# A Nyström attention, an ELU feed-forward and a top-2 expert layer on one core: the written-out order of the work before the experts' weights is replaced

## The chip, the core and the metric

The kernel runs on one core of a Trainium2 chip. The metric is the device time of one execution in microseconds. The core has a matrix engine (PE, with its weight loads shown apart as PEld), a vector engine (DVE), an activation engine (ACT), a general engine (POOL) and SP, which here only issues transfers.

## What is computed

Four batches of eight heads with 576 tokens each go through a Nyström attention with 32 landmarks, then all 2304 tokens through a feed-forward layer with an ELU, then through a noisy top-2 choice of eight experts. Cut to what matters:

```python
q_lm, k_lm = q.reshape(B,H,32,18,64).mean(3), k.reshape(B,H,32,18,64).mean(3)
A, Bm, C = softmax(q @ k_lm.T), softmax(q_lm @ k_lm.T), softmax(q_lm @ k.T)
Z = Bm.T / (norm1(Bm) * norminf(Bm) + 1e-6)
for _ in range(6):
    Z = 2 * Z - Z @ Bm @ Z
x = A @ Z @ C @ v                      # 2304 x 512
h = x @ w_in                           # 512 -> 2048
x = where(h > 0, h, exp(min(h, 0)) - 1) @ w_out
logits = x @ w_gate + log1p(exp(x @ w_noise)) * noise
# the two largest of 8 experts, softmax weights, relu(x @ w1[e]) @ w2[e]
```

## The kernel before

Everything up to the first expert is written as short commands in one long string, `ORDER`; `do` splits it and calls one small function for each word. The string is the program: each engine carries out its instructions in the order in which the words stand, and waits at an instruction until what it needs is there. Nothing reorders them later. The experts 1 to 7 that follow are an ordinary loop and no part of this.

The words are read so. A word with a colon belongs to the attention of one batch, as `1:nm.0` for batch 1. Its stages are the loads (`q`, `k`, `v`; `q.0` is the first four heads), the sums over 18 tokens that make the landmarks (`lmmm`, on PE at line 339 for batch 0), their transposes (`ltr`), the three score products (`asmm`, `bmm`, `csmm`), their softmax steps on DVE, ACT and POOL, and the inverse. The inverse starts with `nmm`, `nval`, `sqmm` and `y0`, then takes five Newton steps: `nm.i` is a product on PE (line 483), `sqout` copies half of it on ACT, `uout` adds the other half on DVE (line 571), and `nm.i+1` needs both. `umm.5` and `uout.5` close it, `ybd` spreads it, `cv` is the product of the third softmax with `v` (line 548), `zcv` (line 582) joins both, and `gmm.0` to `gmm.3` (line 645) multiply that with `w_in`. `ghi` and `glo` store the result as two float16 halves `G`.

The feed-forward layer takes the tokens in six chunks of 512, 256 and four times 384. `L1.c.f` is the first product of chunk `c` and hidden block `f` (line 678, six float16 products). The ELU of one block is five words: `X` (exponential, ACT), `T` (cut at 1 and minus 1, on ACT or DVE), `S` (scale and maximum, DVE, line 706), `H` (first float16 half, ACT), `O` (second half, on DVE or POOL, line 711). `L2.c.f.t` is the second product for 128 tokens (line 718). The last letter of `T` and `O` names the engine:

```python
    if part == "T":
        x.append(S_H if e is V else -S_H)
        if e is V:
            V.tensor_scalar(x[1], x[1], 1.0, 1.0, op0=ALU.min, op1=ALU.subtract)
        else:
            act(x[1], x[1], AF.Relu, scale=-1.0, bias=1.0)
    if part == "O":
        e.tensor_tensor(out=HT[c, f][:, 1], in0=x[1], in1=HT[c, f][:, 0], op=ALU.subtract)
```

`wi` and `Wl` load blocks of `w_in` and `w_out` of 512 KB, and `I.j.0` to `I.j.3`, `Wa`, `Wb` turn them into the number forms that the products use, on ACT, DVE and POOL. `nz`, `cl`, `fill` and `facc` load noise and gate weights and clear two buffers in DRAM. `YA`, `YV` and the words that begin with `R` are the choice of experts, `PD` and `P` load and split the weights of expert 0, and the words that begin with `E`, `W`, `LX` or `X` without the ELU's form are the experts' first stage. `F.n` is a warm-up: `warm(n)` issues products of a constant tile (`hot`) of `n` times 128 columns into a bank that nobody reads, up to 512 columns at a time (line 691). A transfer waits in SP's queue until the buffer that it writes is free and until the transfer eight before it has landed.

Of the kernel before, what the change touches and what calls it, by code (L numbers as in the profile page):

```python
# [56 lines left out]
0:xtp.0.1.0 0:asmax.0 0:bmm I.5.2 Wl.1 0:csmm.0 I.4.3 0:bmax 0:xth.0.1.0 0:xtp.0.1.2 F.16 0:bex 0:csmax.0 wi.14 wi.7
I.3.3 0:assub.0.G 0:bnorm 0:nmm Wa.0.2 F.15 0:nval 0:csexp.0 Wa.1.0 Wa.5.0 Wb.4.0.V F.15 0:xth.1.1.2 Wa.1.1 0:sqmm.0
Wa.5.1 I.1.1 Wa.1.2 I.5.0 0:sqout.0 wi.10 0:xth.0.1.2 nz.3.1 Wa.5.2 0:y0 Wa.1.3 I.7.1 Wl.3 0:csmm.1 F.16 Wa.5.3 F.3
0:xtp.0.1.1 Wa.3.0 0:asexp.0 0:csmax.1 wi.12 0:assum.0 Wa.0.3 nz.1.1 I.14.0 Wb.4.1.V F.9 0:nm.0 0:sqout.1 0:uout.0 wi.8  # L60
0:xth.0.1.1 0:csexp.1 0:etrans.1 0:nm.1 0:sqout.2 Wl.7 0:uout.1 wi.11 Wa.7.0 0:asmm.1 Wl.2 Wa.3.1 0:cssum I.11.0 I.1.0
0:v 0:etrans.2 Wa.3.2 0:etout.2 I.1.2 Wb.0.0.V 0:etrans.0 0:nm.2 0:sqout.3 0:astr.1 0:uout.2 Wa.2.0 nz.3.3 nz.2.2 nz.1.0
0:asmax.1 F.11 1:q.0 0:etout.0 Wb.1.0.V 0:nm.3 0:sqout.4 0:uout.3 0:nm.4 0:sqout.5 nz.3.0 0:asmul.0.G 0:assub.1.V I.10.1
F.9 0:uout.4 I.8.0 I.10.2 I.7.2 Wa.3.3 I.7.0 I.12.0 1:q.1 Wa.2.1 Wa.7.1 Wa.2.2 Wb.1.1.V wi.9 0:etout.1 Wa.2.3 0:umm.5
I.7.3 Wb.3.0.G 0:cv 0:asexp.1 0:asback.0 I.1.3 0:uout.5 1:lmmm.0.0 0:ybd.V 0:cvout 0:assum.1 0:ashi.0 0:zcv 0:asmul.1.G
F.14 0:zout F.8 0:aslo.0.G 0:asback.1 0:gmm.0 0:ghi.0.0 0:ghi.0.1 0:ashi.1 Wa.7.2 0:glo.0.1 0:aslo.1.G I.5.3 1:lmmm.0.1
0:glo.0.0 Wb.0.1.V Wb.2.0.V I.9.0 1:xhi.0.0 1:lmadd.0 Wb.5.0.V L1.0.0 X.0.0 1:v T.0.0.A L1.0.1 1:xlo.0.0 1:k.0 0:gmm.1
wi.13 X.0.1 Wb.3.1.G S.0.0 T.0.1.A H.0.0 wi.15 1:k.1 S.0.1 I.9.1 nz.3.2 L1.0.2 I.8.1 1:lhi.0 O.0.0.V L2.0.0.1 L1.0.3
H.0.1 L2.0.0.3 X.0.2 L2.0.0.0 1:xhi.0.1 I.11.1 L2.0.0.2 cl Wb.2.1.V Wa.7.3 0:ghi.1.1 Wb.5.1.V O.0.1.V 1:xlo.0.1 T.0.2.A
I.9.2 I.9.3 L2.0.1.3 nz.0.1 S.0.2 0:ghi.1.0 1:xhi.1.0 0:glo.1.0 X.0.3 H.0.2 L2.0.1.2 I.8.2 Wl.6 T.0.3.A 0:glo.1.1 S.0.3  # L70
L2.0.1.0 1:lmsum.1.0.V nz.0.2 Wb.7.0.V H.0.3 L2.0.1.1 L1.0.5 O.0.2.G I.8.3 Wb.7.1.V Wa.6.0 1:llo.0 L1.0.4 L2.0.2.2
O.0.3.G 1:xlo.1.0 I.15.0 X.0.4 X.0.5 I.10.0 L2.0.2.3 L2.0.2.0 1:ltr.0 T.0.4.A I.11.2 I.11.3 I.15.1 T.0.5.A S.0.4
1:xtr.0.0 S.0.5 H.0.4 1:lmsum.1.1.V L2.0.2.1 1:lcp.0.A L2.0.3.2 I.10.3 Wl.8 L2.0.3.0 L1.0.6 1:xtr.1.0 Wa.6.1 O.0.4.G
0:gmm.2 H.0.5 L1.0.7 X.0.6 0:ghi.2.1 L2.0.3.1 O.0.5.V 1:lhi.1 I.15.2 T.0.6.A X.0.7 Wa.6.2 0:glo.2.1 0:ghi.2.0 T.0.7.A
nz.0.0 1:xhi.1.1 L2.0.4.2 L2.0.3.3 Wa.8.0 L2.0.4.1 I.15.3 S.0.6 L2.0.5.1 0:glo.2.0 Wa.6.3 nz.0.3 Wb.6.0.V 1:csmm.0
I.14.1 Wa.8.1 1:xlo.1.1 H.0.6 L2.0.4.3 S.0.7 L2.0.5.2 L2.0.4.0 L1.0.9 Wl.12 Wl.9 1:csmax.0 Wb.6.1.V H.0.7 L1.0.8 consts
1:xtr.1.1 O.0.6.G 1:csexp.0 Wa.12.0 L2.0.5.3 L2.0.6.2 I.13.0 L2.0.5.0 1:llo.1 X.0.9 T.0.9.A L2.0.6.0 I.12.1 Wa.9.0
1:ltr.1 Wa.8.2 Wa.12.1 Wl.13 O.0.7.V I.13.1 X.0.8 nz.1.3 Wa.9.1 L2.0.7.2 I.12.2 1:lcp.1.A I.13.2 1:bmm L2.0.6.3 T.0.8.A
I.14.2 L2.0.7.3 I.13.3 Wa.8.3 1:bmax S.0.8 fill.0 Wl.10 1:csmm.1 Wl.11 I.12.3 I.14.3 L2.0.7.0 Wa.9.2 1:csmax.1 Wa.9.3
1:bex 1:csexp.1 Wb.8.0.V L2.0.6.1 H.0.8 Wa.13.0 L1.0.11 1:asmm.0 S.0.9 Wl.14 1:bnorm 1:astr.0 L2.0.7.1 1:etrans.0 1:nmm  # L80
1:nval L1.0.10 Wb.8.1.V 1:etout.0 1:sqmm.0 Wa.10.0 O.0.8.G 1:y0 1:etrans.2 Wb.9.0.V 1:sqout.0 L2.0.8.1 Wa.10.1 H.0.9
# [1343 lines left out]
```

## Time and profile before

| | |
|---|---|
| median of three runs | 785.49 us (784.63 to 786.11) |
| the profiled execution, its own time | 790.36 us |
| its span, first to last instruction | 788.7 us |
| mean granted clock of PE | 0.988 |
| PE busy | 761.0 us, 96% |
| DVE busy | 615.3 us, 78% |
| ACT busy | 427.0 us, 54% |
| POOL busy | 276.1 us, 35% |

The span is the stretch between the first and the last instruction; the execution's own time has a little around it. Busy time is counted from the records of each engine, and a product's recorded end is modelled, so a busy PE can still have small pauses. The granted clock is 1.00 at 2.4 GHz and 0.50 at 1.2 GHz. All times in the rows below count from the start of the span.

### The profile page before, as it was taken

To read this page: it belongs to the slowest core of one execution; us is meant where nothing else is said; L and a number is where in the kernel's file an instruction comes from. 1 tells how busy PE (TensorE), PEld (TensorE's weight loads), DVE (VectorE), ACT (ScalarE), POOL (GpSimd) and SP (SyncE) were. 2 spreads that over 40 slices of the span, in tenths; PEclk is the share of its full clock that TensorE was granted. 3 is DMA by queue.
4 is the path that set the end of the run, shared out by engine and by line. 5 is a ranking of instruction groups with operands and counts; after the bars stand their busy time and mean duration, and the time that the engine had idled before them with its cause. 6 is when DMAs were issued, how large, how long until landed. Compare 5 with 4: busy or idle time off the path is not lost. (4 is left out here: it accounts for less than half of the span.)

```text
span 788.7 us, 17580 instructions
## 1 busy us (share of the span) xinstructions
PE 761.0 (96%) x6991; PEld 447.1 (57%) x6992; DVE 615.3 (78%) x1350; ACT 427.0 (54%) x821; POOL 276.1 (35%) x303
## 2 busy tenths in 40 slices
...
GB/s 342 340 181 213 168 306 213 42 176 186 239 249 135 92 93 52 163 78 99 82 81 105 172 203 134 141 198 44 242 96 220 117 99 224 54 238 27 77 265 65
DMA packets 136200, 123.19 MB, mean 156 GB/s; under 512 B 102891, under 2 KB 105963, under 8 KB 136016
## 3 DMA queue, kind: packets, MB, share of 16 engines
...
## 5 line engine op out<-in xcount | busy, mean ns | idle before, releaser
L718 PE MATMUL y<-wout,g 128*128 128x512 f16 x864 | 205.3, 380 | 0.9 <-DVE g L711 0.8
L1161 PE MATMUL ey<-w,eh 128*128 128x512 f16 x768 | 167.2, 379 | 0.0
L1187 POOL DMA_INDIRECT acc<-eo,tk x35 | 71.1, 2031 | 205.8 <-ACT eo L215 97.5
L718 PEld LDWEIGHTS <-g 128*128 128x128 f16 x864 | 80.6, 98 | 92.3 <-issue 6.5
L1161 PEld LDWEIGHTS <-eh 128*128 128x128 f16 x768 | 75.1, 98 | 89.1
L678 PE MATMUL h<-AT,G 128*128 128x192 f16 (+3 forms) x768 | 108.5, 287 | 2.3 <-DVE e L706 2.2
L678 PEld LDWEIGHTS <-G 128*128 128x128 f16 x768 | 64.1, 98 | 46.6 <-issue 10.6
L711 POOL TENSOR_TENSOR g<-e,g 128x384 f16<-128x384 f32 (+2 forms) x45 | 44.5, 988 | 128.3 <-ACT g L215 118.2
L215 ACT ACTIVATE eh<-c 128x300 f16<-128x300 f32 x112 | 47.7, 453 | 62.9 <-DVE c L1083 58.0
L215 ACT ACTIVATE g<-e 128x384 f16<-128x384 f32 (+2 forms) x96 | 49.2, 520 | 49.8 <-DVE e L706 28.4
L215 ACT ACTIVATE e<-h 128x384 f32<-128x384 f32 (+2 forms) x96 | 46.2, 485 | 42.7 <-PE h L678 20.6
L706 DVE SCALAR_TENSOR_TENSOR e<-e,h 128x384 f32<-128x384 f32 (+2 forms) x96 | 51.6, 548 | 14.2 <-ACT e L215 12.1
L215 ACT ACTIVATE eo<-ey,ws 128x512 f32<-128x512 f32 (+3 forms) x60 | 32.4, 540 | 52.8 <-PE ey L1161 39.7
L903 POOL DMA_INDIRECT xs<-rows,pos x36 | 37.7, 1048 | 53.4 <-DVE mcum L887 25.4
L942 DVE SCALAR_TENSOR_TENSOR w<-ew,w 128x1024 f16<-128x1024 f32 x36 | 43.9, 1243 | 15.8 <-ACT w L215 12.0
L1066 PE MATMUL eb<-tx,wpC 128*128 128x300 f16 x336 | 47.4, 291 | 0.0
L1095 DVE SCALAR_TENSOR_TENSOR eh<-c,eh 128x300 f16<-128x300 f32 x112 | 46.3, 469 | 1.0
L711 DVE TENSOR_TENSOR g<-e,g 128x384 f16<-128x384 f32 (+2 forms) x51 | 30.2, 598 | 18.7 <-ACT g L215 18.4
L1066 PEld LDWEIGHTS <-wpD 128*128 128x128 f16 x336 | 32.8, 98 | 12.1 <-issue 2.0
L1066 PEld LDWEIGHTS <-wpB 128*128 128x128 f16 x336 | 32.9, 98 | 10.0
L1066 PEld LDWEIGHTS <-wpC 128*128 128x128 f16 x336 | 32.8, 97 | 10.1
L1083 DVE TENSOR_TENSOR c<-eb,u 128x300 f32<-128x300 f32 x84 | 37.0, 468 | 0.9 <-PE eb L1066 0.8
...
## 6 DMA issues: line engine op xcount, KB each, us to landing
...
```

The lines of the kernel that those rows point to most:

```text
L215: return A.activation(o, i, f, **kw)
L678: T.matmul(p[:, c0:c0 + n], GT[b, f // 8][:, g, x, fs], AT[b][:, g, y, o:o + n], start=(i == 0), stop=(i == 5))
L706: V.scalar_tensor_tensor(x[1], x[1], x[2], x[0], op0=ALU.mult, op1=ALU.max)
L711: e.tensor_tensor(out=HT[c, f][:, 1], in0=x[1], in1=HT[c, f][:, 0], op=ALU.subtract)
L718: T.matmul(YP[c, t], h[:, x, 128 * t:128 * t + 128], WOUT[f][:, y], start=(f == 0 and i == 0), stop=(f == 15 and i == 2))
L903: n = nc.gpsimd.indirect_dma_start(out=xs[:, :], out_offset=bass.IndirectOffsetOnAxis(ap=R["pos"][:, i // 2, i % 2:i % 2 + 1], axis=0), in ...
L942: V.scalar_tensor_tensor(dst[1][:, ks, :], t, scale, dst[0][:, ks, :], op0=ALU.mult, op1=ALU.subtract)
L1066: T.matmul(p, w_op(e, w, s, k, f), x_op(e, x, t, k), start=(i == 0 and k == 0), stop=(i == 2 and k == 1))
L1083: V.tensor_tensor(out=o, in0=EB[n, f], in1=EU[a, f], op=ALU.add)
L1095: V.scalar_tensor_tensor(lo, o, 0.0, hi, op0=ALU.max, op1=ALU.subtract)
L1161: T.matmul(p, EH[e, f][:, x, 128 * j:128 * j + 128], W2T[e][y][:, f, :], start=start, stop=stop)
L1187: nc.gpsimd.indirect_dma_start(out=acc[:, :], out_offset=bass.IndirectOffsetOnAxis(ap=TK[e][:live(j), j:j + 1], axis=0), in_=EO[e, j], in_ ...
```

## The change

Only the string `ORDER` differs. All words but the warm-ups are the same, and each stands once, so the same arithmetic is done. What differs is the order of the words up to the load and split of expert 0's weights, the engine letter of a part of the `T` and `O` words, and the warm-ups. Sixteen warm-up words of together 226 times 128 columns (60 products) stand before, seven of together 115 (30 products) after: `F.30`, three `F.16`, `F.15`, `F.14`, `F.8`. Of the engine letters, in sum one `T` goes from ACT to DVE and one `O` from POOL to DVE; in the last chunk it is one `T` and two `O`. From `RE.3` in the fifth chunk on, the order of the words is the same but for the engine letters.

```diff
 ORDER = """
-wi.0 F.30 0:k.0 Wl.4 I.0.0 0:q.0 Wa.4.0 F.16 F.16 0:xtp.1.0.0 0:xtp.1.0.2 wi.2 I.0.1 0:xth.1.0.0 I.0.2 0:lmmm.1.0 Wa.4.1
...
+0:q.0 F.30 wi.6 0:xtp.0.0.0 0:k.0 wi.2 wi.0 0:q.1 Wl.4 I.0.1 0:lmmm.0.0 I.2.1 wi.3 0:xtp.1.0.2 F.16 Wa.4.1 0:k.1
...
```

The first place is SP at the start of the program: which transfers are issued first. `k_127`, `q_133`, `q_181`, `k_192` are the four halves of batch 0 before, in this order. First before, then after:

```order
L1238 DMA wi_116<-in_moe_w_in_dram 128x1024
L224 DMA k_127<-in_k_dram 128x1152
L265 DMA wo_129<-in_moe_w_out_dram 128x1024
L224 DMA q_133<-in_q_dram 128x1152
L1238 DMA wi_153<-in_moe_w_in_dram 128x1024
L224 DMA q_181<-in_q_dram 128x1152
L1238 DMA wi_185<-in_moe_w_in_dram 128x1024
L224 DMA k_192<-in_k_dram 128x1152
```

```order
L224 DMA q_116<-in_q_dram 128x1152
L1238 DMA wi_127<-in_moe_w_in_dram 128x1024
L224 DMA k_133<-in_k_dram 128x1152
L1238 DMA wi_135<-in_moe_w_in_dram 128x1024
L1238 DMA wi_137<-in_moe_w_in_dram 128x1024
L224 DMA q_139<-in_q_dram 128x1152
L265 DMA wo_141<-in_moe_w_out_dram 128x1024
L1238 DMA wi_135<-in_moe_w_in_dram 128x1024
L224 DMA k_167<-in_k_dram 128x1152
```

The second half of `k` has moved from the eighth to the ninth transfer, one block of weights further back; the second half of `q` is the sixth in both.

The second place is PE at the end of batch 0's inverse. `nb` holds the Newton products, `l1b` the closing ones (`umm.5` at line 483, `zcv` at line 582), `pcv` is `cv`, the rows at line 339 are landmark sums of batch 1, and `pg` is `gmm.0`. First before, then after:

```order
L483 MATMUL nb_194<-R_570 32x64 x8
L691 LDWEIGHTS hot
L691 MATMUL warm<-hot 128x512
...
L483 MATMUL l1b_159<-R_581 32x32 x8
L548 MATMUL pcv_618<-v_515,ET_559 32x64 x8
...
L339 MATMUL nb_673<-q_557,ident 128x128 x9
L582 MATMUL l1b_159<-Yd_683,CV_685 64x64 x4
L691 LDWEIGHTS hot
...
L645 MATMUL pg_709<-win_131,Z_701 32x512
```

```order
L483 MATMUL nb_145<-R_531 32x64 x8
L548 MATMUL pcv_562<-v_445,ET_515 32x64 x8
...
L483 MATMUL l1b_213<-R_555 32x32 x8
L339 MATMUL nb_654<-q_415,ident 128x128 x9
L582 MATMUL l1b_213<-Yd_650,CV_639 64x64 x4
L339 MATMUL nb_654<-q_550,ident 128x128 x9
L645 MATMUL pg_693<-win_143,Z_676 32x512
```

The product with `v` now stands ahead of `umm.5`, the warm-ups of this stretch are gone but for two that now stand behind `gmm.0`, and the second landmark sum of batch 1 has come ahead of `gmm.0`.

The third place is PE in batch 1's Newton steps, which lie between the feed-forward products of chunk 0 (`h` and `y`). `pa` is `asmm.1`. First before, from the second to the fourth product of the chain, then after:

```order
L431 MATMUL pa_1443<-T_1346,lT_743 32x288
L483 MATMUL pu_1482<-R_1434 32x64 x8
L483 MATMUL pu_1494<-R_1491 32x64 x8
L678 LDWEIGHTS G_956
L678 MATMUL h_13_1505<-AT_690,G_956 128x512
...
L483 MATMUL pu_1516<-R_1503 32x64 x8
```

```order
L678 MATMUL h_12_1427<-AT_553,G_912 128x512
L483 MATMUL pu_1440<-R_1383 32x64 x8
L548 MATMUL pcv_1456<-v_642,ET_1283 32x64 x8
...
L483 MATMUL pu_1517<-R_1453 32x64 x8
L718 LDWEIGHTS g_10_1378
L718 MATMUL y_800<-wout_1130,g_10_1378 128x512
...
L483 MATMUL pu_1551<-R_1532 32x64 x8
```

Two Newton products that stood back to back now have `cv` between them, and the next two have four groups of feed-forward products between them. On DVE, in the same steps, this is what stands between the additions `R` of line 571 that the products wait for; first before, then after:

```order
L571 TENSOR_TENSOR R_1434<-pu_1425,R_1328 128x2x32
L259 TENSOR_SCALAR woc_1244<-wo_1137 128x512
L605 TENSOR_TENSOR ax_1287<-ax_1287,amx_1290 128x576
L260 SCALAR_TENSOR_TENSOR wo_1137<-wo_1137,woc_1244 128x512
L260 SCALAR_TENSOR_TENSOR wo_1220<-wo_1220,woc_1385 128x512
L596 STREAM_TRANSPOSE ax_1478<-pa_1442 128x288
L596 STREAM_TRANSPOSE ax_1478<-pa_1443 128x288
L571 TENSOR_TENSOR R_1491<-pu_1482,R_1434 128x2x32
```

```order
L571 TENSOR_TENSOR R_1383<-pu_1365,R_1315 128x2x32
L601 TENSOR_REDUCE amx_1174<-ax_1171 128x18
L596 STREAM_TRANSPOSE ax_1434<-pa_1399 128x288
L596 STREAM_TRANSPOSE ax_1434<-pa_1400 128x288
L605 TENSOR_TENSOR ax_1171<-ax_1171,amx_1174 128x576
L554 SCALAR_TENSOR_TENSOR cs_1080<-cs_1080 128x2
L555 RECIPROCAL cs_1080<-cs_1080 128x2
L259 TENSOR_SCALAR woc_1360<-wo_1139 128x512
L292 SCALAR_TENSOR_TENSOR wout_1130<-wo_1062,wout_1130 128x512
L260 SCALAR_TENSOR_TENSOR wo_1139<-wo_1139,woc_1360 128x512
L571 TENSOR_TENSOR R_1453<-pu_1440,R_1383 128x2x32
```

The transpose of `pa` (line 596), on which the second product of the chain also waits because it frees a bank, has come from the sixth to the second place behind the first addition, and the weight steps now lie behind it.

## Rows read from the trace of the kernel before

**Rows 1.** The page's first part: engine, busy us, share of span, instructions.

```profile
PE 761.0 (96%) x6991; PEld 447.1 (57%) x6992; DVE 615.3 (78%) x1350; ACT 427.0 (54%) x821; POOL 276.1 (35%) x303
```

**Rows 2.** Windows by stage: stretch, its length, busy us per engine, PE's clock, transfers.

```profile
0.00:57.90 57.90, 48.41 (x535) 32.63 (x537) 36.38 (x98) 30.84 (x67) 21.68 (x25) 0.88 0.90 294
57.90:128.00 70.10, 63.81 (x606) 28.05 (x603) 59.06 (x122) 50.25 (x98) 34.89 (x34) 0.98 0.83 234
128.00:353.60 225.60, 220.94 (x2233) 119.73 (x2234) 169.56 (x457) 135.32 (x299) 86.02 (x115) 1.00 0.52 137
460.00:500.00 40.00, 39.82 (x281) 23.92 (x283) 38.95 (x68) 21.96 (x35) 14.08 (x13) 1.00 0.65 169
```

**Rows 3.** Windows of line 691 alone, the warm-ups: busy us of PE and PEld.

```profile
0.00:57.90 57.90, 16.48 (x60) 5.97 (x60) 0.88 0.90 294
```

**Rows 4.** Timeline of PE, batch 0: start, us, work, [idle before, releaser].

```profile
12.86 2.27 PE L339 MATMUL nb<-q,ident 128*128 128x128 f32 x18
15.58 2.27 PE L339 MATMUL l1b<-k,ident 128*128 128x128 f32 x18 [0.45 <-DMA k<-in_k_dram]
...
44.20 0.44 PE L483 MATMUL l1b<-R 32*32 32x32 f32 x16
46.35 2.79 PE L548 MATMUL pcv<-v,ET 96*32 96x64 f32 x96 [1.72 <-DMA v<-in_v_dram]
49.07 4.09 PE L339 MATMUL nb<-q,ident 128*128 128x128 f32 x18
53.08 0.45 PE L582 MATMUL l1b<-Yd,CV 128*64 128x64 f32 x8
53.47 1.36 PE L691 MATMUL warm<-hot 128*128 128x512 f16 x6
54.76 1.09 PE L645 MATMUL pg<-win,Z 64*32 64x512 f32 x16
...
57.89 3.07 PE L678 MATMUL h<-AT,G 128*128 128x512 f16 x12
```

**Rows 5.** Windows around the low clock, columns as in group 2.

```profile
35.80:39.20 3.40, 3.40 (x41) 1.97 (x26) 2.74 (x8) 2.49 (x6) 1.52 (x2) 0.50 1.00 248
39.20:42.60 3.40, 1.04 (x23) 0.41 (x22) 1.20 (x4) 2.36 (x6) 0.00 (x0) 0.99 1.12 203
42.60:52.90 10.30, 8.59 (x149) 7.35 (x149) 7.72 (x18) 4.89 (x9) 5.63 (x5) 0.50 0.80 226
117.70:121.10 3.40, 3.40 (x24) 1.24 (x23) 2.84 (x9) 1.91 (x5) 0.72 (x1) 0.51 1.05 401
```

**Rows 6.** Timeline of PE, batch 1's Newton products (line 483) and their waits.

```profile
115.87 0.43 PE L483 MATMUL pu<-R 32*32 32x64 f32 x16 [2.04 <-DVE ax L596]
116.89 0.43 PE L483 MATMUL pu<-R 32*32 32x64 f32 x16 [0.60 <-DVE R L571]
...
128.05 0.33 PE L483 MATMUL pu<-R 32*32 32x32 f32 x16 [0.60 <-DVE R L571]
```

**Rows 7.** Timeline of DVE in the same steps.

```profile
114.13 1.29 DVE L260 SCALAR_TENSOR_TENSOR wo<-wo,woc 128x512 int32<-128x512 int32 x2
115.33 0.84 DVE L596 STREAM_TRANSPOSE ax<-pa 128x288 f32<-128x288 f32 x2
...
119.89 0.73 DVE L601 TENSOR_REDUCE amx<-ax 128x18 f32<-128x576 f32 x1
...
121.60 0.75 DVE L605 TENSOR_TENSOR ax<-ax,amx 128x576 f32<-128x576 f32 x1
```

**Rows 8.** What PE waited for from 128.0 to 353.6: us, times, longest.

```profile
PE pu L483 <- DVE R L571: 1.9, 3, 0.7
PE h L678 <- DVE e L706: 1.9, 4, 0.8
```

**Rows 9.** Groups of the ELU's movable parts, 384 columns: busy us, mean ns.

```profile
L711 DVE TENSOR_TENSOR g<-e,g 128x384 f16<-128x384 f32 x34 | 19.5, 581 | 17.2 <-ACT g L215 16.9
L702 DVE TENSOR_SCALAR e<-e 128x384 f32<-128x384 f32 x30 | 12.1, 405 | 11.2 <-ACT e L215 11.1
```

More of the change, by code (lines that the diff above doesn't have):

```diff
@@ L57 @@
[L57 to L81, printed above, removed]
@@ new lines @@
+0:uout.3 Wl.7 0:etout.2 I.7.2 0:sqout.4 I.1.2 0:asexp.1 0:nm.4 I.8.0 1:q.1 nz.0.1 0:ashi.0 0:sqout.5 0:cssum I.5.3
+Wa.2.1 0:cv cl I.8.1 0:uout.4 Wa.3.2 Wa.2.0 Wa.2.2 wi.14 Wb.1.0.V Wb.1.1.V Wa.2.3 wi.15 I.7.0 0:umm.5 0:assum.1 wi.11
+0:cvout I.9.0 1:v 0:uout.5 Wb.5.1.V I.1.3 0:asmul.1.G Wb.0.0.V 0:ybd.V Wa.7.0 1:lmmm.0.0 Wb.2.0.V 0:asback.1 1:xhi.0.0
+0:zcv Wa.3.3 I.10.0 I.7.3 0:zout wi.12 1:xlo.0.0 I.8.2 I.15.0 1:lmmm.0.1 0:gmm.0 1:xhi.0.1 0:ashi.1 0:aslo.0.G 1:lmadd.0
+F.14 0:ghi.0.0 Wa.7.1 0:aslo.1.G F.8 0:glo.0.0 0:ghi.0.1 0:glo.0.1 Wb.3.0.G I.11.1 L1.0.0 L1.0.1 0:gmm.1 Wa.7.2
@@ new lines @@
+1:uout.3 1:asmul.0.G Wb.11.1.G 1:cvout L1.0.14 1:nm.4 H.0.12 1:sqout.5 1:assum.1 2:q.0 L2.0.8.0 L2.0.11.3 Wa.15.2
+O.0.12.V Wa.14.1 Wa.15.0 Wb.13.0.V L2.0.12.1 1:uout.4 X.0.14 3:k.0 1:asmul.1.V L2.0.12.3 1:umm.5 Wa.14.2 Wb.13.1.V
+H.0.13 Wa.14.0 L2.0.12.0 L2.0.12.2 1:uout.5 Wa.14.3 1:ybd.A 2:q.1 1:asback.1 1:zcv T.0.14.A Wb.14.0.G S.0.14 1:zout
+L2.0.11.1 O.0.13.G L2.0.13.2 Wa.15.3 L2.0.11.0 1:asback.0 L2.0.11.2 H.0.14 1:ashi.0 1:gmm.0 X.0.15 1:aslo.0.V 1:ashi.1
+1:ghi.0.0 L2.0.13.3 T.0.15.A Wb.14.1.G O.0.14.G 1:ghi.0.1 Wb.15.0.V L2.0.13.0 2:v S.0.15 1:glo.0.0 1:glo.0.1 L2.0.14.1
@@ new lines @@
+T.2.10.A L1.2.12 L2.2.8.0 S.2.10 2:assub.1.G RK.1 H.2.10 X.2.12 L2.2.9.1 RF.1 3:lhi.0 T.2.12.A S.2.12 2:nm.3 O.2.10.V
+2:asexp.1 L1.2.11 2:asmul.0.V L2.2.8.1 L2.2.10.1 L1.2.13 X.2.11 2:uout.3 2:sqout.4 L2.2.9.2 3:llo.0 T.2.11.A S.2.11
+2:nm.4 H.2.12 2:asback.0 2:uout.4 2:sqout.5 facc.2 L2.2.9.0 2:umm.5 L2.2.10.0 L1.2.14 H.2.11 2:uout.5 O.2.12.G 2:ashi.0
+2:ybd.V 2:zcv O.2.11.V L2.2.11.2 PD.0.7 X.2.13 2:zout L2.2.12.0 2:gmm.0 X.2.14 3:xtr.1.0 2:ghi.0.1 L2.2.11.0 2:assum.1
+T.2.14.A 2:asmul.1.V 3:ltr.0 T.2.13.V 3:lmsum.1.1.G RS.1.0 S.2.13 L2.2.10.2 L2.2.11.1 2:asback.1 2:aslo.0.V 2:ghi.0.0
```

206 lines of the change are left out of this document (108 added, 98 removed).

## The prediction, made blind

> **What bounds the kernel now.** I read the page first: PE is busy 96% of the span, DVE 78% [rows 1]. That share mixes stages, so the windows come next [rows 2]. They fall into three parts. Up to the first feed-forward product (57.9 us) PE is idle 9.5 us, and 16.5 of its 48.4 busy us are warm-ups whose result nobody reads [rows 2, 3]. So 26 us of this stage are no work, and the stage is as long as one chain: loads of batch 0, landmarks, inverse, first feed-forward product. From 57.9 to 128.0 PE is idle 6.3 us of 70.1. From 128.0 to 353.6 it is idle 4.7 of 225.6: there the kernel is bound by PE, and an order can win only a few us. Behind that the windows have next to no idle PE, and the order is the same.
>
> Two more views say what the idle time is. The timeline of PE shows which product waited and for whom [rows 4, 6], and the windows around the low clock show what the waits cost a second time: between 39.2 and 42.6 PE is busy 1.04 us of 3.4, and the clock then stands at 1.2 GHz up to 52.9 [rows 5]. In that stretch the landmark sum of nine products takes 4.09 us; at 2.4 GHz it takes 2.27 [rows 4]. The stretch at 117.7 is of the same kind, and it follows the waits of batch 1's Newton steps [rows 5, 6].
>
> **First stage, the warm-ups and the chain.** Thirty of 60 warm-up products go, 111 of 226 units. As columns they are worth half of the busy time in group 3, some 6 us at full clock (22 units took 1.36 us, 0.06 each [rows 4]). But they stand where PE waits for the chain, so most of their time turns into idle time. What counts is when the chain gets there, and I walk it in four steps.
>
> Loads: with 4.46 MB issued up to it, the eighth transfer let the last landmark sum start at 15.58; the sixth (3.34 MB) let another start at 12.86 [rows 4]. That is 0.41 MB per us. The last half of `k` is now ninth, 0.52 MB later: 1.3 us, so about 16.9. But in the new order two sums stand together behind the wait for the second half of `q` (12.9 as before), and each takes about 2.0 us from start to start: 12.9, two, 0.7 of transposes, two, two, 19.6, against 17.7 before. The chain is 1.9 us late here.
>
> Up to `umm.5`: three `F.16` stood between the sums and the first small score product, some 2.6 us by their units; they are gone there, so the product comes 0.7 us earlier. Its softmax and the start of the inverse then stand behind more weight steps on DVE and lose that again. The five Newton steps wait for DVE and ACT, whose work did not shrink. I take `umm.5` where it was, at 44.2 [rows 4].
>
> From `umm.5` to the first feed-forward product, before: `cv` waited 1.72 us for `v`, started at 46.35, took 2.79 us, the landmark sum behind it 4.09, and `zcv` started at 53.08 [rows 4]. After: `cv` stands ahead of `umm.5`, and `v` has some 10.8 MB ahead of it in SP's queue in place of 12.9. So `zcv` waits for DVE instead. Behind the last Newton addition stand there three weight steps of 0.65 us each, a softmax sum (0.73 and two short ones), the addition, one more weight step and the spread: about 4.9 us by the durations of [rows 7]. That puts `zcv` at 49.0, 4.1 us earlier. Between it and `gmm.0` a landmark sum (2.27 us) stands in place of the warm-ups (1.36), so `gmm.0` comes at 51.4 instead of 54.76, and the feed-forward product 3.1 us behind it as before: 54.6 instead of 57.89, a gain of 3.3.
>
> The clock takes part of it back. While PE waits for the second half of `q`, from about 9.9 to 12.9, there is now little for it to do, much as between 39.2 and 42.6 before [rows 5]; I take one sum at 1.2 GHz, 1.2 us (the bounds are 0 and 1.8, the difference of 4.09 and 2.27 [rows 4]). And the stretch from 36 on, with fewer warm-ups, will be at 1.2 GHz again, as it was; where it now reaches another sum, up to 1.8 more. I take 0.6. The first stage: 3.3 less 1.8, **1.5 us gained** (bounds 3.3 gained and 1 lost).
>
> The clock fell behind a stretch in which PE was busy 1.04 us of 3.4 [rows 5], and by that row I count low-clock time only behind stretches as empty as this one. [...]
>
> **Second stage, batch 1's inverse among chunk 0.** Before, the second Newton product waits 2.04 us for a transpose on DVE that stood behind four other instructions; the third and the last wait 0.60 each for the addition, since they stand right behind the product before [rows 6]. The low clock that follows costs half of 3.4 us, 1.7 [rows 5]. Together 4.9. After, the transpose is second behind the addition, and every pair of Newton products has other work between. New waits come. Between the first two additions DVE now has a reduction, two transposes, a subtraction and two weight steps, at least 0.73 + 0.84 + 0.75 + 1.29 = 3.6 us, and short ones [rows 7]; PE has behind the transpose only the product and `cv`, some 1.9 of the 3.1 us that DVE still needs there. That is a wait of 1.3. And a first feed-forward product now waits for a bank that DVE frees behind a softmax sum: about 1.5. So 4.9 less 2.8, and of the other waits of this stage (6.3 idle in all [rows 2], of which 3.2 are counted) I take back 1.3, since the first chunk's `L1` and `L2` and the small score product of batch 1 have more between them and what they wait for. **3.4 us gained** (bounds 6 gained, 1 lost).
>
> **Third stage.** PE waited 1.9 us in three steps for the same additions and 1.9 for the ELU [rows 8]. Two of the back-to-back pairs of batch 2 are gone too (1.3), and many `L2` of the second and third chunk stand nearer to their `L1` (I put 0.8 against it). **0.5 gained** (bounds 3 gained, 3 lost).
>
> **The ELU parts.** In sum DVE gets one `T` of 0.41 us and one `O` of 0.58 [rows 9]. In the last chunk it is 1.6 us, and DVE is busy 38.95 of 40 us from 460 to 500 [rows 2]. PE has 0.18 us idle there, so the cover is its own queue; without it the cost is 1.6. I take 0.
>
> **Sum.** 1.5 + 3.4 + 0.5 = 5.4 us. The profiled execution took 790.36, so 785.0 for it; the median of the runs is 785.49, 4.9 below the profiled one, so the forecast for the median is **780.1**.
>
> **Rivals.** One: the gains are larger. The clock holds in the first stage (3.3), the second gives back the 6 us of idle and low clock, and the third is equal: 9.3, 776.2. For it: with the waits spread out there is less reason for the low clock. Against it: DVE is busy 59.1 of 70.1 us in the second stage [rows 2], so its queue ends some waits late whatever PE's order is.
>
> Two: nothing comes of it. The warm-ups turn to idle time, and the waits of batch 1 move elsewhere: DVE's 11 us of idle time in the second stage stay. The chain was as long as DVE and ACT made it: 785.5.
>
> Three: the low clock holds through the first stage. Beyond the 1.8 already taken, both sums behind the first (1.4), the Newton products (1.0), `cv`, the sum and `gmm.0` of the end (3.5) run at 1.2 GHz: 5.9 us. With the other stages as forecast it is 786.0, and it is the first product at about 62 that would show it.
>
> Four, the other sign: the ELU of the second chunk becomes the bound. In 12 of its 16 blocks fewer products stand between `L1` and the first `L2` than before; the least are worth 3.3 us where it was 4.6, and the five ELU words of a block, at about 0.5 us each [rows 9], need some 2.5 with every queue free. If ACT or DVE are behind there, each of the twelve waits as long as the longest wait for this in the third stage, 0.8 [rows 8]: 9.6 us, 789.7. It decides from nine such waits on.
>
> **How the numbers follow.** Forecast 0.42, rival one 0.20, two 0.15, three 0.10, four 0.13. A measurement of this kernel tells about 0.2%, 1.6 us, from no change. The forecast and the first rival are faster, but for 0.02 of the forecast's lower bounds, which are the same; of rival two 0.04 is faster; the third is the same or slower, half each. So faster 0.64, same 0.18, slower 0.18. The range goes from a little below the first rival, 775.5, to 787.5, between the third and the fourth; it leaves out most of the fourth and the far ends of the bounds.
>
> **What would show it.** Right: the first product of line 678 at 55 to 57.5; `zcv` waiting for DVE and no more behind `cv`; the last product of batch 1's chain some 5 us ahead of 128.05; no wait over 1.6 us at line 483 between. Wrong: the first product behind 58 with a long stretch at 1.2 GHz; waits of line 718 for `g` in the second chunk that add up to several us; or as much idle time in the second stage as before, at other places.

## The result and the profile after

| | before | after |
|---|---|---|
| median of six runs | 785.06 us | 777.44 us (775.56 to 779.94) |
| ratio, 95% interval | | 0.9905 (0.9883 to 0.9927) |
| profiled execution, its time and span | 790.36, 788.7 us | 779.94, 778.3 us |

The change saves 7.6 us by the medians and 10.4 by the two profiled executions. The forecast was 5.4, 780.1 us. The profiled execution of the changed kernel is the slowest of its six, 2.5 us above their median. To see where the time went, the page's first part and the windows by stage of the changed kernel come first. The stages end at the first feed-forward product, at the first product of chunk 1, at chunk 5 and at the end. The mark for chunk 5, here as in [rows 2], is the first product of the second block that it takes, 0.98 us behind its very first product. Columns are as in [rows 2].

```profile
PE 754.0 (97%) x6961; PEld 445.0 (57%) x6962; DVE 618.4 (79%) x1352; ACT 427.1 (55%) x820; POOL 281.9 (36%) x302
```

```profile
0.00:56.36 56.36, 44.04 (x504) 31.11 (x506) 40.68 (x100) 32.24 (x69) 24.33 (x26) 0.85 0.94 304
56.36:131.53 75.17, 73.49 (x693) 32.78 (x692) 68.94 (x141) 60.02 (x118) 45.98 (x42) 1.00 0.74 200
131.53:339.88 208.35, 207.13 (x2146) 114.03 (x2145) 158.30 (x436) 124.62 (x278) 74.00 (x106) 1.00 0.59 154
339.88:778.30 438.42, 429.29 (x3622) 267.11 (x3619) 350.48 (x678) 210.22 (x358) 137.63 (x131) 1.00 0.55 134
```

The same windows of a second execution of the kernel before (the first experiment below), between the same four products:

```profile
0.00:54.56 54.56, 46.07 (x534) 30.62 (x536) 37.08 (x98) 31.00 (x67) 21.65 (x25) 0.94 0.94 312
54.56:135.79 81.23, 75.02 (x699) 32.61 (x696) 70.33 (x142) 59.44 (x117) 41.81 (x39) 0.98 0.75 218
135.79:347.27 211.48, 208.69 (x2149) 114.86 (x2143) 159.15 (x437) 126.18 (x280) 79.01 (x110) 1.00 0.55 139
347.27:780.70 433.43, 427.65 (x3621) 266.70 (x3619) 350.40 (x676) 210.49 (x359) 132.91 (x131) 1.00 0.55 136
```

Length against length, the changed kernel is 1.8 us longer in the first stage, 6.1 shorter in the second and 3.1 shorter in the third, and then 5.0 longer in the last, where not one word has moved. The second stage wins twice: PE's idle time falls from 6.2 to 1.7, and its busy time by 1.5, since no stretch at half clock (a granted 0.50) is left in it (mean clock 1.00 for 0.98). The third wins 1.6 us of idle time, from 2.8 to 1.2, and 1.6 of busy time at the same clock, for a reason that no view here shows. Neither trace of before is the typical one: [rows 2] begin feed-forward 3.3 us later than this one, and their third stage holds some 2 us more idle time.

Here is PE at the end of batch 0's inverse, after, for [rows 4]:

```profile
42.74 0.65 PE L483 MATMUL nb<-R 32*32 32x64 f32 x16 [0.87 <-ACT R L215]
43.34 2.79 PE L548 MATMUL pcv<-v,ET 96*32 96x64 f32 x96
46.06 0.44 PE L483 MATMUL l1b<-R 32*32 32x32 f32 x16
46.43 2.79 PE L339 MATMUL nb<-q,ident 128*128 128x128 f32 x18
51.55 0.45 PE L582 MATMUL l1b<-Yd,CV 128*64 128x64 f32 x8 [2.34 <-DVE Yd L378]
51.94 2.27 PE L339 MATMUL nb<-q,ident 128*128 128x128 f32 x18
54.14 1.09 PE L645 MATMUL pg<-win,Z 64*32 64x512 f32 x16
55.16 1.36 PE L691 MATMUL warm<-hot 128*128 128x512 f16 x6
```

`zcv` waits for DVE, as expected, and no more behind `cv`. But `umm.5` comes at 46.06, 1.9 us later than before. It needs the last addition (line 571), and that waits for the half that ACT copies. ACT, then DVE:

```profile
44.32 0.69 ACT L215 ACTIVATE wi<-wi 128x512 int32<-128x512 uint32 x1 [1.06 <-DMA wi<-in_moe_w_in_dram]
44.91 0.68 ACT L215 ACTIVATE AT<-ay 128x576 f16<-128x576 f32 x1
45.49 0.21 ACT L215 ACTIVATE R<-nb 128x64 f32<-128x64 f32 x1
45.73 0.23 DVE L571 TENSOR_TENSOR R<-nb,R 128x64 f32<-128x64 f32 x1 [0.98 <-ACT R L215]
```

The copy stands behind a weight step whose block of `w_in` had not landed. The `cv` that was put ahead of `umm.5` on PE ends at the same time as the addition, so it costs nothing here. And PE in batch 1's Newton steps, for [rows 6]:

```profile
105.86 0.42 PE L483 MATMUL pu<-R 32*32 32x64 f32 x16
109.65 0.43 PE L483 MATMUL pu<-R 32*32 32x64 f32 x16
111.84 0.43 PE L483 MATMUL pu<-R 32*32 32x64 f32 x16 [0.29 <-DVE R L571]
114.89 0.43 PE L483 MATMUL pu<-R 32*32 32x64 f32 x16
116.34 1.46 PE L678 MATMUL h<-AT,G 128*128 128x512 f16 x6 [1.02 <-DVE e L706]
...
119.36 0.43 PE L483 MATMUL pu<-R 32*32 32x64 f32 x16
122.41 0.33 PE L483 MATMUL pu<-R 32*32 32x32 f32 x16
```

The 2.04 and the two 0.60 of before are gone, and the chain ends at 122.41, 5.6 us ahead of 128.05. Last, PE near the end, in the last expert:

```profile
746.74 0.39 PE L1161 MATMUL ey<-w,eh 128*128 128x512 f16 x1
750.58 1.83 PE L1161 MATMUL ey<-w,eh 128*128 128x512 f16 x4 [3.44 <-issue]
```

```profile
746.70:750.50 3.80, 0.43 (x3) 0.10 (x1) 0.00 (x0) 1.66 (x4) 0.00 (x0) 1.00 0.66 209
750.50:754.00 3.50, 3.42 (x9) 1.27 (x10) 0.00 (x0) 0.00 (x0) 0.00 (x0) 0.53 0.37 134
```

PE stands still for 3.44 us in the middle of one accumulation, for nothing that the profile shows, and then runs 3.4 us at half clock: products of 512 columns start 0.427 us apart in it and 0.216 us behind it. The profile gives the clock as a share alone; the 1.2 and 2.4 GHz of the forecast agree with these two rates, 1.2 and 2.4 columns a ns. As an estimate from them, half of the 3.4 us at half clock is lost: 3.4 and 1.7, some 5.1 for the 5.0 of the last stage.

### The profile page after: what moved, and what is told of

It reads as the page before. It is cut to its first block, busy times and chain, and to the rows that moved or that the text cites. A ratio compares the mean times of both kernels' runs of the same rounds, so it can differ in the third digit from the quotient of the medians.

```text
span 778.3 us, 17519 instructions
## 1 busy us (share of the span) xinstructions
PE 754.0 (97%) x6961; PEld 445.0 (57%) x6962; DVE 618.4 (79%) x1352; ACT 427.1 (55%) x820; POOL 281.9 (36%) x302
## 3 DMA queue, kind: packets, MB, share of 16 engines
q1 hardware_dynamic: 125392, 100.67, 47.2%
## 5 line engine op out<-in xcount | busy, mean ns | idle before, releaser
L1161 PE MATMUL ey<-w,eh 128*128 128x512 f16 x768 | 169.1, 382 | 3.4 <-issue 3.4
L1187 POOL DMA_INDIRECT acc<-eo,tk x35 | 74.2, 2121 | 202.1 <-ACT eo L215 90.5
L215 ACT ACTIVATE eo<-ey,ws 128x512 f32<-128x512 f32 (+3 forms) x60 | 32.5, 541 | 64.0 <-PE ey L1161 50.9
L215 ACT ACTIVATE w<-ew 128x1024 f16<-128x1024 f32 x36 | 37.0, 1050 | 0.2
## 6 DMA issues: line engine op xcount, KB each, us to landing
wi<-in_moe_w_in_dram SPq DMA_DIRECT2D x16, 512.0 KB, 10.3
```

Source lines behind the costliest of these rows:

```text
L215: return A.activation(o, i, f, **kw)
L1161: T.matmul(p, EH[e, f][:, x, 128 * j:128 * j + 128], W2T[e][y][:, f, :], start=start, stop=stop)
L1187: nc.gpsimd.indirect_dma_start(out=acc[:, :], out_offset=bass.IndirectOffsetOnAxis(ap=TK[e][:live(j), j:j + 1], axis=0), in_=EO[e, j], in_ ...
```

## The experiments

The string takes other numbers of lines in these kernels, so their line numbers are 28 to 31 higher: 706 to 709 is line 678, 734 to 737 line 706, 511 to 514 line 483, 1189 and 1197 are 1161 and 1167. The diffs show only some of the words that differ, and the lines of the string are broken otherwise there. Ratios are to the kernel before, run on the same chip; between two of them they are divided. The kernel before took 784.4 us on the chip of the first four kernels here, 787.9 on that of the three with other warm-ups and of the new order with the old letters, 788.0 on that of the 45 products, of the old order with the new letters and of the Newton steps, and 787.0 on that of the last. So lengths of traces from two of these chips can differ by some us for that alone.

**The kernel before again.** No edit.

> The kernel before, unchanged, as a control. Its profiled execution of group 1 was 4.9 us above the median of its runs, so the idle time read there may hold some chance waits. Theory A (the order sets the waits, and the extra time lies anywhere): the median stands within 0.2% of the kernel before, and the new trace has the first product of line 678 again at 57 to 58.5, the last product of batch 1's Newton chain at 127 to 129, and chunk 5 beginning at 353 to 354.5. Theory B (part of the idle time of the second and third stage in that trace was chance): chunk 5 begins 3 to 5 us earlier, near 349 to 350, with less idle time at line 678 and 444 in the third stage.

Measured: ratio 0.9999 (0.9986 to 1.0012). The profiled execution, the shortest of twelve but one, had the first product of line 678 at 54.56, the chain's end at 124.57 and chunk 5 at 347.27. It is theory B, and more: of the 788.7 us 8.0 are not there in this execution, 3.3 of them in the first stage, 2.9 in the third and 1.6 in the last. The pattern of batch 1's waits, 2.04 and twice 0.60, came again to the hundredth.

**The stages apart.** Three kernels take one order up to a word and the other behind it, without the words already done:

```diff
 ORDER = """
-wi.0 F.30 0:k.0 Wl.4 I.0.0 0:q.0
+0:q.0 F.30 wi.6 0:xtp.0.0.0 0:k.0 wi.2
...
 L1.0.0 X.0.0 T.0.0.A L1.0.1 1:k.0 0:gmm.1 X.0.1 Wb.3.1.G S.0.0
...
```

This is the first of them, with the new start and the old rest.

> The new order up to the first feed-forward product, the old order for all words that are then left. Theory A (each stage keeps its own gain): the first product of line 678 at 56 to 56.8, and of the 7.6 us of the whole change 1.5 stay, 783.5 (ratio 0.998). Theory B (the start is where the gain comes from, since the old order behind it was only late because it began late): ratio 0.993 or less, 780 or less. Theory C (chunk 0 eats it, as the third product of line 678 was only 0.34 us earlier in the changed kernel): no change, 785.

> The new order up to the first product of chunk 1 (batch 1's inverse among chunk 0 included), the old order behind it. Theory A: first and second stage keep their gains and the third is worth little, as predicted (1.5, some 6 and 0.5): 777.5 to 778.5, ratio 0.991, and chunk 1 begins near 131.5. Theory B (the third stage is worth what the two profiled executions show, 6.0 us from the first product of chunk 1 to that of chunk 5): 781 to 783, with chunk 5 beginning 5 to 6 us later than in the changed kernel.

> The old order with all sixteen warm-ups up to the first feed-forward product, the new order for all words that are then left. Theory A (stages add up): the first product of line 678 at 57.9, and all but 1.5 us of the gain stays, 779, ratio 0.992; no stretch at 1.2 GHz behind 58, since the pairs of Newton products of batch 1 stand apart. Theory B (the gain comes from the start and the fewer warm-ups): 783 or more, ratio above 0.997.

Measured: new start and old rest 1.0071 (1.0048 to 1.0094), 5.6 us slower than before; new up to chunk 1 0.9964 (0.9945 to 0.9983); old start and new rest 0.9974 (0.9958 to 0.9990). All theories on the sum of stages fall: in the first kernel the new start costs where it should save, and in the third the new rest saves 2 us of 7.6. Against the second trace of before, on the same chip, the first kernel's second stage is 2.3 us longer and its last one 2.6; the latter has the pause of the changed kernel, 2.44 us. What is left are waits of PE behind the seam, first with the old start and the new rest, then with the new start and the old rest, with what ACT did ahead of the latter:

```profile
PE h L707 <- DVE e L735: 6.1, 1, 6.1
```

```profile
65.23 4.67 PE L707 MATMUL h<-AT,G 128*128 128x512 f16 x12 [6.12 <-DVE e L735]
```

```profile
62.81 2.72 PE L706 MATMUL h<-AT,G 128*128 128x512 f16 x6 [4.18 <-DVE e L734]
```

```profile
60.23 0.67 ACT L243 ACTIVATE wi<-wi 128x512 int32<-128x512 uint32 x1 [3.38 <-DMA wi<-in_moe_w_in_dram]
```

A feed-forward product waits for the bank that DVE's ELU step frees. The weight steps and loads that the one order had left for later, and the other wants done, stand ahead of that step: with the old start DVE itself is behind, and with the new one DVE waits for ACT's exponential, which stands behind a weight step that waits 3.38 us for its block of `w_in`. Behind the seam the third stages come out as in the whole kernels: 208.64 us with the new order and the old start, 211.47 with the old order and the new start. The second kernel, with its seam at chunk 1, had 76.16 us in the second stage and 210.19 in the third, and its median of 781.6 is that of its theory B. But chunk 5 begins 3.2 us later than in the changed kernel, not the 5 to 6 of that theory.

**The number of warm-up products and the pause.** Three kernels. The first cuts the same columns into more products, the second takes nine warm-ups out of the kernel before, the third puts nine back into the changed one:

```diff
-F.30
+F.1 F.1 F.1 F.1 F.1 F.1
...
-F.16
+F.1 F.1 F.1 F.1 F.1 F.1 F.1 F.1 F.2 F.2 F.2 F.2
```

```diff
-F.16 F.16 0:xtp.1.0.0
+F.16 0:xtp.1.0.0
...
-F.11 0:nm.3
+0:nm.3
```

```diff
-0:lmmm.0.1
+F.16 F.16 0:lmmm.0.1
...
-0:nm.0
+F.16 F.3 F.9 0:nm.0
```

> The changed kernel, with the same warm-up columns (115 units of 128) cut into 60 products in place of 30: the first warm-up into thirty products of 128 columns, the second into eight of 128 and four of 256. Both stand where PE waits for loads. The three traces of kernels with 30 warm-up products so far all have a pause of 2.4 to 3.4 us at the same product of an expert, the 95th or 94th from the end of PE's program (line 1161 of the changed kernel), which waits for nothing that the profile shows, and 1.2 GHz behind it; the three with 60 products have none. Theory A (fewer instructions ahead of the experts move the code of that product against the pieces of 16 KB in which it is fetched): the pause is gone, the stretch from the last first-stage product of expert 0 to the end takes 335 to 337 us in place of 340.4, and the median is 773 to 774.5. Theory B (the pause is chance, or comes from the new order's transfers): 777.4, with the pause in its place.

> The kernel before without nine of its sixteen warm-ups (30 products, 111 units), the seven that stay being those of the changed kernel's sizes. Theory A (as in the first text: code position): the pause of some 3 us at the 95th or 94th product from the end appears, and the median is 787 to 789. Theory B (warm-ups only turn into idle time): 784 to 785, no pause. Theory C (the warm-ups' columns lay on the path, or hold PE at 2.4 GHz): the first product of line 678 up to 2 us earlier (columns on the path), or later than 57 with more than 14 us at 1.2 GHz ahead of it (clock).

> The changed kernel with the nine warm-ups put back at comparable places, ahead of the products of batch 0 that wait longest. Theory A (they fill idle time, and their only other effect is the position of the experts' code): the first product of line 678 at 55 to 57, no pause at line 1161, median 773 to 775. Theory B (fewer warm-ups are the gain, their columns being on the path): 779 or more, the first product of line 678 behind 58. Theory C (with them the clock stays at 2.4 GHz up to the first feed-forward product): less than 7 us at 1.2 GHz in the first stage, against 17 in the changed kernel, and that product at 54 or before.

Measured: 0.9920 (0.9904 to 0.9937), 1.0004 (0.9993 to 1.0016) and 0.9905 (0.9892 to 0.9918). The pause went and came as theory A says: none in either kernel with 60 products, 1.86 us at the 95th product from the end in the kernel before with 30. The times don't follow it. The last stage became 433.7 and 433.4 us, 5 shorter, but the third is 4.4 and 5.5 longer than in the changed kernel's trace. Some 3 us of that is a second pause, in batch 3's first Newton product, which took 0.36 us there; here it is in the first of the three:

```profile
265.83 0.33 PE L514 MATMUL pu<-R 32*32 32x64 f32 x4 [1.11 <-issue]
266.58 0.21 PE L514 MATMUL pu<-R 32*32 32x64 f32 x1 [0.42 <-issue]
267.28 0.21 PE L514 MATMUL pu<-R 32*32 32x64 f32 x1 [0.49 <-issue]
```

The rest may be the chip: the kernel before with nine warm-ups less, run on the same one, has 213.9 us in the third stage, where the other two have 212.7 and 213.9. In that kernel the pause came without its price: the last stage is 437.3 us, but the median did not move, as theory B has it. What won the time back isn't shown. Its first product of line 678 came at 54.84, with a mean clock of 0.84 up to there.

The pair of the changed kernel with 60 products also bears on what the clock of the first stage costs. Windows up to the first product of line 678, all work and then the warm-ups alone (PE, PEld), first with the warm-ups cut finer, then with nine put back:

```profile
0.00:55.53 55.53, 43.63 (x535) 34.09 (x537) 40.77 (x100) 32.24 (x69) 24.16 (x26) 0.85 0.93 309
0.00:55.53 55.53, 8.66 (x60) 5.55 (x60) 0.85 0.93 309
```

```profile
0.00:55.60 55.60, 46.82 (x535) 31.61 (x537) 40.56 (x101) 32.21 (x69) 25.25 (x26) 0.94 0.96 316
0.00:55.60 55.60, 16.11 (x60) 5.87 (x60) 0.94 0.96 316
```

With the clock taken as 1.00 or 0.50 alone, as the windows of [rows 5] have it, a mean of 0.85 is 16.7 us at half clock (2 x 0.15 x 55.53), 0.94 is 6.7. The stage is 0.07 us apart. Theory C is half right: with the nine warm-ups the mean clock is 0.94 for 0.85, and the first product comes no earlier. But the pair changes two things, since the nine warm-ups are also 7.5 us more of PE's own work (16.11 for 8.66). So it doesn't price the clock.

Five traces bear on it better, whose warm-ups and chain have the same order up to that product: the two of the kernel before, and these three (old start with new rest, where only some weight steps and loads come in between; old order with new letters; Newton steps alone):

```profile
0.00:55.02 55.02, 45.68 (x534) 30.80 (x536) 36.42 (x98) 30.98 (x67) 21.66 (x25) 0.94 0.98 321
0.00:55.90 55.90, 47.08 (x535) 31.39 (x537) 37.07 (x98) 30.95 (x67) 21.67 (x25) 0.91 0.93 304
0.00:56.65 56.65, 47.24 (x535) 31.95 (x537) 36.49 (x98) 30.98 (x67) 21.68 (x25) 0.91 0.91 300
```

Clocks of 0.94, 0.94, 0.91, 0.91 and 0.88 go with first products at 54.56, 55.02, 55.90, 56.65 and 57.89. By the same sum that is 6.5 us at half clock in the first and 13.9 in the last, 7.4 more, and the products lie 3.3 us apart: near half. Less half of the time at half clock, an estimate from these five, the first product comes at 50.9 to 51.7 in these five and at 46.1 in the kernel before with nine warm-ups less; in the pair it comes at 47.2, and at 52.3 with nine put back. So by this estimate nine warm-ups cost some 5 us ahead of the first product, and the higher clock that goes with them (0.94 for 0.85 in the pair) gives back as much.

**Forty-five products.**

```diff
-F.30
+F.1 F.1 F.1 F.1 F.1 F.1 F.1 F.1
+F.1 F.1 F.1 F.1 F.1 F.1 F.1 F.1
+F.2 F.2 F.2 F.2 F.2 F.2 F.2
```

> The changed kernel with the first warm-up cut into 23 products (sixteen of 128 and seven of 256 columns) in place of 8, so that there are 45 warm-up products in all; the columns are the same. With 30 products every trace so far had the pause at line 1161 near the end (five of five), with 60 none (five of five), but both kernels with 60 products and the new order had 3.3 us of another pause in batch 3's first Newton product. Theory A (both come from where pieces of code begin, and 45 meets neither): 772 to 774 where the kernel before takes 785, ratio 0.985. Theory B (the code of one of the two places is met again at 45): 0.990 to 0.992, with one of the two pauses in the trace. Theory C (the pauses have nothing to do with the number of products): as the changed kernel, 0.9905.

Measured: 0.9968 (0.9946 to 0.9989), worse than the changed kernel. The trace has both pauses, theory B and more. The one near the end:

```profile
756.98 0.23 PE L1197 MATMUL ey<-w,eh 128*32 128x128 f16 x1 [2.27 <-issue]
```

This product is the 110th from the end: fifteen products more ahead, and the pause is fifteen earlier in the code. It is the 95th in five kernels with 30, the 94th in a sixth. With 60 the same count from the start is the 125th from the end; there the changed kernel cut finer has 0.22 us of the same kind, and the other six show none. So by these counts this pause hangs on the position in the code. The other does not: it is at the same product, the 4277th from the end, with 45 and with 60.

**The engine letters.** The T and O words keep their places, 88 of 192 change the letter:

```diff
-O.0.3.V O.0.5.G T.1.0.A
+O.0.3.G O.0.5.V T.1.0.V
...
```

> The changed kernel with the engine letters of before in all T and O words (88 words differ, in sum one T and one O fewer on DVE). Theory A (the prediction: the parts are hidden behind PE's own queue): 777.4 within 1.6 us. Theory B (the letters were fitted to the new order, so the old ones put ELU parts on an engine that is busy there): 780 or more, with waits of line 718 for g or of line 678 for e. Theory C (DVE is what the last chunk waits for): 775.5 or less, since DVE has two O and one T fewer there.

> The kernel before with the engine letters of the changed kernel in all T and O words (88 words differ). The other way round, the new order with the old letters, took 1.5% more than the new order with its own. Theory A (the letters fit an order, each its own): slower than the kernel before, 1.005 to 1.02, with waits of line 678 for e and of line 718 for g in the stages of chunk 0 to 3. Theory B (the new letters are simply the better choice): 0.99 to 0.995. Theory C (they matter only under the new order): 1.000 within 0.002.

Measured: the new order with the old letters 1.0051 (1.0034 to 1.0069), which is 1.5% above the changed kernel; the old order with the new letters 1.0101 (1.0077 to 1.0126). Theory B of the first and theory A of the second. Second and third stage of the new order with the old letters:

```profile
56.48:133.91 77.43, 73.91 (x693) 32.77 (x693) 70.83 (x142) 60.42 (x118) 44.85 (x41) 1.00 0.73 195
133.91:352.84 218.93, 210.99 (x2146) 114.62 (x2145) 156.07 (x436) 125.66 (x278) 78.20 (x108) 1.00 0.55 146
```

PE's idle time is 3.5 and 7.9 us there, 1.7 and 1.2 with the letters of the change. It lies in many waits of at most 1.1 us. This trace has the pause near the end too, as it has 30 products.

**Of the change only the Newton steps of batch 1, in the old order.**

```diff
-1:uout.0 Wa.13.1 L2.0.9.3 1:assub.0.V 1:asmm.1 Wa.10.3 H.0.11 2:k.1 Wa.13.2 Wa.11.2 X.0.12 Wa.13.3 1:astr.1 1:nm.1 1:sqout.2 1:uout.1 1:nm.2 1:sqout.3 L1.0.13
+1:uout.0 1:asmm.1 1:astr.1 L2.0.9.3 Wa.13.1 1:assub.0.V Wa.10.3 H.0.11 2:k.1 1:nm.1 1:sqout.2 1:uout.1 Wa.13.2 Wa.11.2 X.0.12 Wa.13.3 L1.0.13 1:nm.2 1:sqout.3
...
-L2.0.10.0 X.0.13 Wb.11.1.G L2.0.10.3 1:nm.4 1:sqout.5 1:uout.4 2:q.1 1:asexp.1 1:assum.0 1:umm.5
+X.0.13 Wb.11.1.G 1:nm.4 1:sqout.5 1:uout.4 2:q.1 1:asexp.1 1:assum.0 L2.0.10.0 L2.0.10.3 1:umm.5
```

> The kernel before, with one part of the change alone: in batch 1's Newton steps the transpose of the second score half comes directly behind its addition on DVE, one group of four L2 products comes between that score product and the second Newton product, L1 of block 13 between the second and the third Newton product, and two groups of L2 between the last two. Theory A (these waits and the 1.2 GHz behind them are what the second stage loses, 4.9 us by the prediction): the last product of the chain 4 to 5 us after fewer us from the first product of line 678 than the 70.0 of the control (65 to 66), no stretch at 1.2 GHz between 100 and 130, and 780 to 781 on a chip where the kernel before takes 785 (ratio 0.9945). Theory B (DVE is what bounds this stage: it has as much to do as before, so the waits come back behind): the chain's end earlier by 2 or more, but the first product of chunk 1 less than 1.5 earlier, ratio 0.998 or more.

Measured: 0.9974 (0.9961 to 0.9988), between the two. The chain ended 67.2 us behind the first product in place of 70.0, no stretch at half clock stood between 100 and 130, and the second stage took 77.92 us, 3.3 shorter. Not all went, since DVE comes late one step on:

```profile
115.02 0.42 PE L512 MATMUL pu<-R 32*32 32x64 f32 x16
117.52 0.42 PE L512 MATMUL pu<-R 32*32 32x64 f32 x16 [2.07 <-DVE R L600]
```

**A shorter chain in the first stage.** In the changed kernel 62 words at the end of batch 0's inverse are put in another order, and the two warm-ups of that place go ahead to the loads:

```diff
-0:nm.4 I.8.0 1:q.1 nz.0.1 0:ashi.0 0:sqout.5 0:cssum I.5.3 Wa.2.1 0:cv cl I.8.1 0:uout.4 Wa.3.2
+0:nm.4 0:sqout.5 I.8.0 1:q.1 nz.0.1 0:ashi.0 0:uout.4 0:cssum I.5.3 I.1.3 Wa.2.1 0:umm.5 0:cv cl
+0:uout.5 0:ybd.V 0:assum.1 0:cvout I.8.1 0:aslo.0.G Wa.3.2
...
```

> The changed kernel with 62 words at the end of batch 0's inverse in another order, and the two warm-ups ahead of the first feed-forward product (22 units, six products) set 45 us earlier, where PE waits for the second half of q, so that the number of warm-up products is as in the changed kernel. The closing copies and additions of the inverse come ahead of the weight steps on ACT and DVE, umm.5 ahead of cv, the spread and the steps of the attention weights that POOL does ahead of its weight steps, gmm.0 between the two landmark sums of batch 1. Theory A (the first stage is the chain of batch 0, as predicted): zcv at 47 to 49 in place of 51.55, the first product of line 678 at 53.3 to 54 in place of 56.36, and 2 to 3 us of that reach the end: 774.5 to 775.5 where the changed kernel takes 777.4, ratio to the kernel before 0.987. Theory B (behind 57 the stage is bound by DVE and ACT, which have the same work to do): the first product comes early, but line 678 then waits for e, the third product of line 678 at 61 to 62 as in the changed kernel, and the median is 776.8 to 778, ratio 0.990. Theory C (the weight steps put off stop the second products of chunk 0): 779 or more.

Measured: 0.9969 (0.9951 to 0.9987), 5 us slower than the changed kernel. `zcv` came at 46.77 and the first feed-forward product at 54.08, as theory A has it, and then theory C: the wait below is what the chain had won. PE, and the window behind:

```profile
54.08 2.75 PE L706 MATMUL h<-AT,G 128*128 128x512 f16 x12
...
61.00 4.17 PE L706 MATMUL h<-AT,G 128*128 128x512 f16 x12 [3.15 <-DVE e L734]
```

```profile
60.00:75.00 15.00, 14.00 (x62) 6.17 (x62) 15.00 (x23) 12.42 (x23) 11.14 (x13) 0.89 0.60 159
```

DVE is busy 15.00 of 15.00 us there. The second stage became 79.0 us in place of 75.2. The third has 213.0, with the pause in batch 3's first Newton product.

## Why the prediction came near, point by point

**The sum** was 5.4 and came out at 7.6, inside the range. It did so by terms that erred in both directions: 1.5, 3.4, 0.5 and nothing behind were forecast; by the second trace of before they were -1.8, 6.1, 3.1 and -5.0, by the first 1.5, 6.2, 6.0 and -3.3. These add up to 2.4 and 10.4, so single traces don't close to the 7.6 of the medians. That the sum came near is in part luck.

**First stage.** The change gains nothing here that can be told from chance. The old start put the first product of line 678 at 57.89, 54.56, 55.02, 55.90 and 56.65 in the five traces that have it unchanged, the new one at 56.36, 54.40, 56.75 and 56.48 in four: means of 56.0 and 56.0. The 1.5 that agreed with the first pair was luck. Three steps failed. "I take `umm.5` where it was" overlooked ACT's queue: the last Newton product came at 42.74 against 42.57, as said, but the copy behind it stood behind a weight step that waited for its transfer, so `umm.5` came at 46.06 in place of 44.20. Then "about 4.9 us" to `zcv` was 5.5. And "most of their time turns into idle time" put the warm-ups that went at nothing, where by the estimate above nine warm-ups are worth some 5 us to the chain and as much, the other way, by the clock. A gain of this stage need not last either: in the last experiment the first product came 2.3 us earlier, and a product in chunk 0 waited 3.15 for DVE, busy 15.00 of 15.00 us from 60 on.

**The clock of the first stage.** I took off 1.8 for it, and the traces speak for such a price. By [rows 5] the low stretch covered `cv` and the landmark sum (4.09 us) in that execution; the next one has no room for a stretch of that length (10.3 us), with 6.5 us at half clock in the whole stage by its mean clock of 0.94. The 3.3 us between 57.89 and 54.56 go with that: 13.9 us at half clock in the one, 6.5 in the other, with three more traces of the same start in line between them. After the change the mean clock is 0.85, some 17 us. Half of the time at half clock, as I priced the 3.4 us in the second stage, was an estimate from the granted 0.50. The five traces agree with it, with 3.3 us for 7.4, though no run changes the clock alone. Rival three falls all the same: it put the first product at about 62, and without nine warm-ups ahead of it that came at 56.36.

**Second stage.** The mechanism was right, and its size too small. The chain's end came 5.6 us ahead of 128.05 ("some 5" was said), and no wait at line 483 is above 0.29. The new waits were mis-sized: 1.3 at the third Newton product measured 0.29, and 1.5 for the bank measured 1.02. The rest of the stage's idle time, of which I took 1.3 back, went nearly all. That is 6.1 to 6.2 for 3.4, and it is no chance: the stage took 80.6 to 81.4 us in three traces with the old order and warm-ups or nine less, and 74.7 to 76.2 in five with the new start, order and letters. The edit of the Newton steps alone gave 3.3 us in the stage and 2.0 at the end. Rival two falls: this idle time did not come back in the third stage.

**Third stage.** 0.5 forecast, 3.1 against the second trace of before. There is no wait of line 718 for `g` beyond 0.2 us, so rival four did not come. Why it did not is the next point. The waits of [rows 8] are gone, but it is not a gain that can be told from chance: in four of five other kernels that have this order and these letters there the stage took 212.7 to 216.9 us, with a pause in batch 3's first Newton product and others. Six traces with the new order there have a mean of 212.2 us, six with the old one 212.4. Whether other executions of the changed kernel have that pause is open, since one was profiled.

**The ELU parts.** "0", from the sums of one `T` and one `O`, held for the last chunk: from the mark for chunk 5 to the product of `RG.5` 59.61 us after, 59.92 before. But it was the wrong question. Eighty-eight letters move, and with the old ones the new order loses 1.5%, more than the whole gain. The letters belong to the terms of stage two and three; order and letters won't come apart.

**Behind the common words** I had zero, "the order is the same". It was -5.0, and this is the largest miss. The thirty products that went, each with a weight load, also moved all later code of PE. The page lists transfers of instructions on their own (`q8 instruction: 56, 0.92, 0.5%`, so 16 KB each); whose code they hold it doesn't say. In the second trace of the kernel before, one of them starts 4.6 us ahead of the 95th product from the end; in the changed one none starts behind the one at 726.0, at product 367 from the end, until PE has stood still for 1.1 us, and then two do, at 748.2 and 751.6. In the 3.9 us up to the last product ahead of the pause PE takes 144 short ones. That PE waits for its code is argued from this; shown is that the pause, of 1.9 to 3.4 us, came in all seven traces of kernels with 30 or 45 products, on four chips, at these places in none of seven with 60, and moved by fifteen products with fifteen.

**Rival one**, larger gains at 776.2, came nearer to 777.4 than the forecast did. Its second stage (6.0) is right; its first is not, and nobody counted the loss in the last stage.

**What stays open:** how the terms of the stages make 7.6, and the pause at batch 3's first Newton product. It is at one product with 45 and with 60 warm-up products, and the kernel with the old start and the new rest has it not, with as many instructions as those that have it. But the chip is a rival there: the five traces that have the pause, all with the new order, are from the three chips on which the kernel before takes 787.0 to 788.0 us, and that kernel ran on the one where it takes 784.4; the chip of the changed kernel, which has it not either, is not on record. No run tells the two apart.
